# Second K and Q pieces on the SP and ACT queues, V first on GpSimd's queue, and a last row block in three column parts

## The chip, the core and the metric

The kernel runs on one core of a Trainium2 chip. The core has five engines with an instruction list each, taken in order: TensorE (PE; its weight loads are shown as PEld), VectorE (DVE), ScalarE (ACT), GpSimd (POOL) and SyncE (SP). They wait for one another by semaphores. Loads and stores are carried by 16 DMA engines that all queues share. GpSimd's queue is a software one (its instruction writes the descriptors and keeps it busy); the SP and ACT queues are hardware ones. The metric is the device time of one execution in microseconds, median of several.

## What is computed

A sliding-window attention over 8 batches, 8 heads, 576 tokens and head size 64, then a feed-forward layer with squared ReLU over its 4608 rows of 512:

```
scores = q @ k.T / 8,  masked to |i - j| <= 32
attn   = softmax(scores);  x = attn @ v          # heads side by side: 4608 x 512
h      = x @ w_in                                # 4608 x 2048
out    = (max(h, 0) ** 2) @ w_out                # 4608 x 512
```

Inputs and output are float32 in HBM; the matmuls run in bf16.

## The kernel before

The class `Gen` records operations, and the class `Prog` orders them. `Prog.rec` notes an operation's engine, its function, what it reads and writes, a sort key, a duration guessed in ns (`dur`), and for a transfer its packets (`move`: packets per DMA engine, ns of each, extra latency). `Prog.schedule` runs a list-scheduling model (`forward`, L98) forward and backward under several settings, keeps the best order, and `emit` writes one list per engine. So a changed duration or a changed key can move any operation of any engine. Operations with keys at or below -100 keep the order of their keys; the loads at the start have such keys, from the string `ORDER` (L34), in which `k01` is piece 1 of K of batch 0, `w10` the first quarter of `w_in` and `w20` that of `w_out`.

`fill` (L306) puts matmuls of zeros (L409) into the gaps that the plan has on TensorE up to about 30 us; `EXTRA` more of them stand before the first matmul of the first layer, which in the plan waits for `w10`.

Attention. K, Q and V come in pieces of tokens (`PIECE0`, L38, for K and Q of batch 0: 96, 64, 128, 128, 128, 32 tokens; `PIECE`, L39, for V). `tok_load` (L455) issues a K or Q piece on GpSimd's queue, float32 to bf16 on the way, 8 packets per token; `vx_load` (L526) does so for V. Piece 0 of K and Q of batch 0 is different: `first_load` (L448) issues it as float32 on the SP and ACT queues into two output buffers that are free then. `tok_turn` (L465) transposes a piece on TensorE into a PSUM bank and copies it to bf16 in SBUF, K by VectorE, Q by ScalarE; the float32 piece is transposed in float32 with a float32 identity, made by VectorE (L414) from an IOTA of GpSimd (L412). `scores`, `av`, `evac` and `xturn` then do a chunk of 64 tokens: scores, exponential, mask, weighted V, division, and the transpose of the result into `XT`. For the first eight chunks TensorE does these steps with one or two chunks at a time.

Feed-forward. `load_w1` (L544) and `load_w2` (L549) issue the weights in quarters on GpSimd's queue. `mm1_small` (L756; matmuls at L766) multiplies 128 rows by a quarter of `w_in` in 16 matmuls of 128 columns; `mm1_half` and `mm1` do wider ones later. ScalarE applies the ReLU and VectorE squares. `mm2` (L846) multiplies a block of 128 rows by `w_out` in four segments of 4 matmuls, ScalarE copies the 512 columns out of PSUM, and ACT's queue stores them. The last of the 36 row blocks goes to `last` (L825): two halves of 256 columns in two segments of 8 matmuls each; the first half is copied by ScalarE and stored by ACT's queue, the second copied by VectorE and stored by SP's:

```
        h, s = divmod(seg, 2)
        op, tag = ((self.OUTP[1][:, 0:256], ("outp", 1)), (self.BK["A"][:, 0:256], "sA"))[h]
```

GpSimd's list at the start is: IOTA, k01, q01, v00, v01, k02, q02, v02, w10, k03, q03, v03, k04, q04, v04, w11, w12, w13 and so on.

Of the kernel before, what the change touches and what calls it, by code (L numbers as in the profile page):

```python
# [19 lines left out]
VS = D_ + 2  # L20
KW = 32 + S_ + 32
LEAD = 12
WARM, COLD, DENSE, SPARSE, EXTRA = 36000, 8000, 1.15, 0.95, 16
NPE = 18
TB, TX = 1, 5
TOFF, TST = 6, 0.9
# [4 lines left out]
PADS, MARGINS, ROUNDS, NREP = (0, 1000, 2000), (0, 4000, 8000), 3, 4  # L31
LATE = {"POOL": 1500, "SP": 2000, "ACT": 2000}
DEPTH, POST, BACK = 4000, {"POOL": 1500, "SP": 1000, "ACT": 1000}, {"POOL": 2500, "SP": 4000, "ACT": 4000}
ORDER = ("k01 q01 v00 v01 k02 q02 v02 w10 k03 q03 v03 k04 q04 v04 w11 w12 w13 k05 q05 k10 q10 v10 k11 q11 v11 "  # L34
         "w20 w21 w22 w23 k12 q12 v12 k13 q13 v13 k14 q14 v14").split()
GT0, WT0 = (12.5, 16, 20, 25.5), (13, 18, 23, 26)
TURN0 = {1: 1, 2: 2, 4: 3, 6: 4}
# [10 lines left out]
class Prog:  # L48
# [49 lines left out]
    def forward(self, key=None, seq=None, rnd=None, pad=0):  # L98
# [3 lines left out]
        ready = [0.0] * n  # L102
        start, end = [0.0] * n, [0.0] * n
        free = {e: 900.0 for e in ENGS}
        free["POOL"] = 1350.0
        wait = {e: [] for e in ENGS}
        pool = {e: [] for e in ENGS}
        at = {e: 0 for e in ENGS}
# [250 lines left out]
class Gen:  # L359
# [5 lines left out]
    def alloc(self):  # L365
        nc = self.nc
        sb, ps = nc.alloc_sbuf_tensor, nc.alloc_psum_tensor
        self.SC = ps("sc", [128, 2048], F32)
        self.BK = {x: self.SC[:, 512 * i:512 * i + 512] for i, x in enumerate("ACBD")}
        self.TRP = self.BK["D"].bitcast(BF16)  # L370
        self.HT = [ps(f"ht{i}", [128, 512], F32) for i in range(2)]
        self.OUTP = [ps(f"outp{i}", [128, 512], F32) for i in range(2)]

        self.RAW = {t: [sb(f"{t}raw{i}", [128, 2560], BF16) for i in range(2)] for t in "qk"}
        self.QT = [sb(f"qt{i}", [128, 4, S_], BF16) for i in range(2)]
        self.KT = [sb(f"kt{i}", [128, 4, KW], BF16) for i in range(2)]
        self.VD = [sb(f"vd{i}", [128, 4, H_, VS], BF16) for i in range(2)]
        self.KA = [sb(f"ka{i}", [128, 4, 3, 128], BF16) for i in range(2)]
        self.VX = [sb(f"vx{i}", [128, 5, H_, VS], BF16) for i in range(2)]
        self.MASK = sb("mask", [128, 64], BF16)  # L380
        self.MASK2 = sb("mask2", [128, 2, 64], BF16)
        self.IOTA = sb("iota", [128, 256], mybir.dt.int32)
        self.IDW = sb("identw", [128, 256], BF16)
        self.ID = self.IDW[:, 64:192]
        self.MK = sb("mk", [128, 64], F32)
        self.E = sb("e", [128, 2048], BF16)
        self.PT = sb("pt", [128, 3 * 768], BF16)
        self.RS = [sb(f"rs{i}", [128, 16], F32) for i in range(4)]
        self.XR = sb("xr", [128, 4, 512], BF16)
        self.PF = sb("pf", [128, 16 * VE], F32)  # L390
        self.XT = sb("xt", [128, 4, NTOK], BF16)
        self.W1 = sb("w1", [128, 4, DFF], BF16)
        self.W2 = sb("w2", [128, 16, DM], BF16)
        self.GT = [sb(f"gt{i}", [128, 16, 512], BF16) for i in range(2)]
        self.RT = [sb(f"rt{i}", [128, 512], BF16) for i in range(4)]
        self.ZZ = sb("zz", [128, 128], BF16)
        self.OE = [sb(f"oe{i}", [128, 512], F32) for i in range(4)]
        self.STG = {"k": (self.OE[0], ("oe", 0)), "q": (self.OE[1], ("oe", 1))}
        self.IDF = self.OE[3][:, 0:128]


# [8 lines left out]

    def setup_masks(self, key):
        self.p.rec("POOL", lambda e: e.iota(self.IOTA[:], [[1, 256]], base=0, channel_multiplier=-1), writes=["iota"],  # L412
                   key=key, dur=400)
        self.p.rec("DVE", lambda e: e.tensor_scalar(self.IDF, self.IOTA[:, 0:128], 0.0, None, ALU.is_equal),  # L414
                   reads=["iota"], writes=[("oe", 3)], key=key - 0.1, dur=200)
        self.p.rec("DVE", lambda e: e.tensor_scalar(self.IDW[:], self.IOTA[:], 64.0, None, ALU.is_equal),
                   reads=["iota"], writes=["id"], key=key, dur=330)
        self.p.rec("DVE", lambda e: e.tensor_scalar(self.MK[:], self.IOTA[:, 0:64], -64.0, None, ALU.is_ge),
                   reads=["iota"], writes=["mk"], key=key + 0.1, dur=130)
        self.p.rec("DVE", lambda e: e.scalar_tensor_tensor(self.MASK[:], self.IOTA[:, 0:64], 0.0, self.MK[:], ALU.is_le,  # L420
                                                           ALU.mult),
                   reads=["mk", "iota"], writes=["mask"], key=key + 0.1, dur=130)
        self.p.rec("DVE", lambda e: e.tensor_scalar(self.MASK2[:, 0, :], self.IOTA[:, 0:64], -64.0, None, ALU.is_le),
                   reads=["iota"], writes=[("mask2", 0)], key=-20, dur=130)
        self.p.rec("DVE", lambda e: e.tensor_scalar(self.MASK2[:, 1, :], self.IOTA[:, 0:64], 0.0, None, ALU.is_ge),
                   reads=["iota"], writes=[("mask2", 1)], key=-20, dur=130)
# [18 lines left out]
    def slot(self, b, x):  # L445
        return 512 * (x if b else x - 1)

    def first_load(self, t, eng, key):  # L448
        t0, n = PIECE0[0]
        src = (self.q if t == "q" else self.k)[0, :, t0:t0 + n, :].rearrange("h p d -> p h d")  # L450
        stg, tag = self.STG[t]
        dst = bass.AP(stg, 0, [[512, n], [64, 8], [1, 64]])
        self.p.rec(eng, lambda e: e.dma_start(dst, src), writes=[tag], dma=(f"s{t}", 0), key=key, dur=420, move=(n // 2, 14, 1500))

    def tok_load(self, b, t, x, key):  # L455
        t0, n = self.pieces(b)[x]
# [2 lines left out]
        y = x - 1 if not b else x  # L459
        self.p.rec("POOL", lambda e: e.dma_start(dst, src), writes=[("fraw", b, t, x)], old=[("fraw", b - 2, t, y + (b == 2))],  # L460
                   reads=self.pace(b, x, "kqv".index(t)), dma=(f"f{b % 2}{t}{y}", b), key=key,
                   dur=500 + 3.2 * n, move=(n // 2, 13.3, (0, 1500, 800, 800, 800, 800)[x] if b == 0 else 200))
        self.p.ops[-1].slack = SLACK if b >= FB else 0

    def tok_turn(self, b, x, key):  # L465
        t0, n = self.pieces(b)[x]
        early = b == 0 and x < 3
        first = b == 0 and x == 0
        if b == 0 and x == 1:
            parts = [(t, "s" + u, self.BK[u].bitcast(BF16)) for t, u in ("kB", "qD")]  # L470
        elif early:
            parts = [(t, ("ht", u), self.HT[u][:] if first else self.HT[u][:].bitcast(BF16)) for u, t in enumerate("kq")]
        elif b:
# [8 lines left out]
        def f(e, todo):  # L482
            for t, tag, ps in todo:
                for j in range(4):
                    src = bass.AP(self.STG[t][0], 128 * j, [[512, n], [1, 128]]) if first else bass.AP(
                        self.RAW[t][b % 2], self.slot(b, x) + 128 * j, [[2560, n], [1, 128]])
                    mm = e.transpose(ps[:, 128 * j:128 * j + n], src, self.IDF[0:n, 0:n] if first else self.ID[0:n, 0:n])  # L487
            return mm

        for todo in ([parts[:1], parts[1:]] if early else [parts]):  # L490
            rd = [self.STG[t][1] for t, _, _ in todo] + [("oe", 3)] if first else [("fraw", b, t, x) for t, _, _ in todo]
            self.p.rec("PE", lambda e, a=todo: f(e, a), reads=rd + ["id"],
                       writes=sorted({tag for _, tag, _ in todo}), key=key, dur=450 if first else 240 * len(todo), att=True)
        if b == 0 and x == 3:
# [49 lines left out]
    def load_w1(self, d, key):  # L544
        src = self.w_in[:, 512 * d:512 * d + 512].rearrange("(f p) c -> p f c", p=128)
        self.p.rec("POOL", lambda e: e.dma_start(self.W1[:, :, 512 * d:512 * d + 512], src),  # L546
                   writes=[("w1", d)], dma=(f"w1{d}", 0), key=key, dur=770, move=(32, 82, 500))

    def load_w2(self, d, key):  # L549
        src = self.w_out[512 * d:512 * d + 512, :].rearrange("(k p) c -> p k c", p=128)  # L550
# [273 lines left out]

    def last(self, seg, key):  # L825
        gt = self.GT[(NT - 1) % 2]
        h, s = divmod(seg, 2)
        op, tag = ((self.OUTP[1][:, 0:256], ("outp", 1)), (self.BK["A"][:, 0:256], "sA"))[h]

        def f(e):  # L830
            for d in range(8 * s, 8 * s + 8):
                mm = e.matmul(op, gt[:, d, 384:512], self.W2[:, d, 256 * h:256 * h + 256], start=(d == 0), stop=(d == 15))  # L832
            return mm

        self.p.rec("PE", f, reads=[("gt", (NT - 1) % 2, d, 3) for d in range(8 * s, 8 * s + 8)] + [("w2", 2 * s), ("w2", 2 * s + 1)],
                   writes=[tag], key=key, dur=854)
        if s:
            oe = self.OE[3 * h][:, 0:256]
            if h:
                self.p.rec("DVE", lambda e: e.tensor_copy(oe, op), reads=[tag], writes=[("oe", 3)], key=key, dur=330)  # L840
            else:
                self.p.rec("ACT", lambda e: e.activation(oe, op, ACTF.Copy), reads=[tag], writes=[("oe", 0)], key=key, dur=400)
            self.p.rec("SP" if h else "ACT", lambda e: e.dma_start(self.out[NTOK - 128:NTOK, 256 * h:256 * h + 256], oe),
                       reads=[("oe", 3 * h)], writes=[("out", -h)], dma=(f"oz{h}", 0), key=key, dur=400, move=(8, 50))

    def mm2(self, T, u, seg, key):  # L846
        x = 4 * T + u
# [41 lines left out]
    def build(self):  # L889
# [18 lines left out]
        for b in range(B_):  # L908
# [2 lines left out]
                tile += 1  # L911
            if b < FB:
                if not b:
                    self.first_load("k", "SP", -300)
                    self.first_load("q", "ACT", -300)
                for bb in range(0 if b else FB):
                    for x in range(6):
                        for t in "kqv":
# [105 lines left out]
```

## Time and profile before

| | us |
|---|---|
| median of 6 runs (lowest, highest) | 303.65 (302.44, 304.67) |
| the profiled execution's own time | 304.46 |
| its span, first to last instruction | 302.6 |
| TensorE busy | 294.7 (97%) |
| VectorE, ScalarE, GpSimd busy | 177.9, 159.5, 106.7 |
| first piece of K, of Q landed (hardware queues) | 4.13, 4.44 |
| k01, q01, v00, v01 landed | 4.93, 5.35, 6.70, 7.81 |
| k02, q02, v02 landed | 8.98, 10.22, 11.10 |
| w10 issued, landed | 7.07, 16.34 |
| k03, q03, w11, w12, w13 landed | 17.19, 18.07, 23.77, 26.30, 28.85 |
| last matmul ends, last store issued | 300.02, 300.61 |

Times count from the span's start. A load has landed when the last of its 16 completions, one per DMA engine, has come. In the profile's lines, "x16" counts instructions, "out<-in" names what is written and read by the program's names without buffer numbers, and the bracket at the end of a line of the timeline gives the idle time of the engine before it and what ended it. The granted TensorE clock was 0.999 over the span. A busy TensorE includes the matmuls of zeros (120 in this execution, all before 15 us).

### The profile page before, as it was taken

To read this page: it belongs to the slowest core of one execution; us is meant where nothing else is said; L and a number is where in the kernel's file an instruction comes from. 1 tells how busy PE (TensorE), PEld (TensorE's weight loads), DVE (VectorE), ACT (ScalarE), POOL (GpSimd) and SP (SyncE) were. 2 spreads that over 40 slices of the span, in tenths; PEclk is the share of its full clock that TensorE was granted. 3 is DMA by queue.
4 is the path that set the end of the run, shared out by engine and by line. 5 is a ranking of instruction groups with operands and counts; after the bars stand their busy time and mean duration, and the time that the engine had idled before them with its cause. 6 is when DMAs were issued, how large, how long until landed. Compare 5 with 4: busy or idle time off the path is not lost.

```text
span 302.6 us, 7056 instructions
## 1 busy us (share of the span) xinstructions
PE 294.7 (97%) x2786; PEld 172.0 (57%) x2786; DVE 177.9 (59%) x429; ACT 159.5 (53%) x266; POOL 106.7 (35%) x133
## 2 busy tenths in 40 slices
PE   8869999999999999999999999999999999999996
PEld 8759965775858764544544444444454444444444
DVE  6666657754998966658566496758447663222200
ACT  3356644574747645754565674647464554444311
POOL 8999914240604631552055544315510000000000
PEclk9999999999999999999999999999999999999999
DMA  9999999999999999999899999999992310100022
GB/s 111 152 187 176 200 179 174 175 135 163 186 156 134 140 169 160 143 129 146 152 130 131 151 168 160 124 175 95 163 161 72 87 26 35 37 35 36 35 96 79
DMA packets 166673, 39.07 MB, mean 129 GB/s; under 512 B 157808, under 2 KB 162160, under 8 KB 166640
## 3 DMA queue, kind: packets, MB, share of 16 engines
q0 software_dynamic: 115200, 18.16, 89.3%
q1 hardware_dynamic: 45472, 10.96, 24.5%
q10 hardware_dynamic: 5968, 9.51, 10.3%
q8 instruction: 22, 0.36, 0.5%
q14 instruction: 11, 0.09, 0.1%
HBM read 36.70 MB, written 9.44 MB: 152 GB/s over the span
## 4 chain that ended last, share of the span: by engine, by line
PE 91%; POOL 4%; DMA 4%; issue 0%; DVE 0%; DVEq 0%; POOLq 0%
PE outp L855 40%; PE ht L807 28%; PE ht L789 7%; PE ht L766 7%; DMA w<-in_moe_w_in_dram 4%; PE sc L643 3%; PE sc L583 3%; POOL vx L529 1%; POOL kraw L460 1%; POOL qraw L460 1%; PE sc L487 1%; PE sc L832 1%; PE outp L832 1%; PE sc L691 0%; POOL w L546 0%
## 5 line engine op out<-in xcount | busy, mean ns | idle before, releaser
L855 PE MATMUL outp<-w,gt 128*128 128x512 bf16 x560 | 136.0, 379 | 0.0
L807 PE MATMUL ht<-xt,w 128*128 128x512 bf16 x384 | 94.5, 379 | 0.0
L822 DVE TENSOR_TENSOR gt<-rt 128x512 bf16<-128x512 bf16 x144 | 59.1, 418 | 58.0 <-ACT rt L813 50.9
L813 ACT ACTIVATE rt<-ht 128x512 bf16<-128x512 f32 x96 | 57.3, 599 | 56.7 <-PE ht L807 54.6
L855 PEld LDWEIGHTS outp<-w,gt 128*128 128x128 bf16 x560 | 52.7, 98 | 58.3 <-DVE gt L822 0.2
L807 PEld LDWEIGHTS ht<-xt,w 128*128 128x128 bf16 x384 | 36.5, 98 | 42.4
L460 POOL DMA_DIRECT2D qraw<-in_q_dram x40 | 34.7, 868 | 53.6 <-DVE xr L667 12.7
L460 POOL DMA_DIRECT2D kraw<-in_k_dram x40 | 34.9, 873 | 43.0 <-PE ht L807 19.1
L603 ACT ACTIVATE e<-sc 128x512 bf16<-128x512 f32 (+1 forms) x48 | 37.4, 810 | 11.5 <-PE sc L583 11.5
L529 POOL DMA_DIRECT2D vx<-in_v_dram x40 | 34.7, 868 | 19.0 <-PE ht L807 11.6
L862 ACT ACTIVATE oe<-outp 128x512 f32<-128x512 f32 x35 | 20.9, 598 | 26.7 <-PE outp L855 26.6
L667 DVE TENSOR_TENSOR xr<-pf,rs 128x512 bf16<-128x512 f32 (+1 forms) x42 | 27.7, 681 | 0.4
L766 PE MATMUL ht<-xt,w 128*128 128x128 bf16 x384 | 24.1, 219 | 2.4 <-DMA w<-in_moe_w_in_dram 2.0
L624 DVE TENSOR_TENSOR pt<-e,mask 128x512 bf16<-128x512 bf16 x42 | 17.6, 421 | 13.9 <-ACT e L603 13.8
L789 PE MATMUL ht<-xt,w 128*128 128x256 bf16 x192 | 23.4, 273 | 0.0
L766 PEld LDWEIGHTS ht<-xt,w 128*128 128x128 bf16 x384 | 21.7, 98 | 3.0 <-issue 1.7
L774 ACT ACTIVATE rt<-ht 128x512 bf16<-128x512 f32 x24 | 14.2, 599 | 13.3 <-PE ht L766 13.1
L660 DVE COPY pf<-sc 128x520 f32<-128x520 f32 x21 | 14.7, 698 | 11.1 <-PE sc L643 10.9
L789 PEld LDWEIGHTS ht<-xt,w 128*128 128x128 bf16 x192 | 18.0, 98 | 3.3
L657 ACT ACTIVATE pf<-sc 128x520 f32<-128x520 f32 x21 | 12.6, 600 | 12.3 <-PE sc L643 11.0
L795 ACT ACTIVATE rt<-ht 128x512 bf16<-128x512 f32 x24 | 14.4, 599 | 7.5 <-PE ht L789 6.8
L662 DVE TENSOR_TENSOR pf<-pf 64x520 f32<-64x520 f32 x21 | 14.6, 697 | 5.5 <-ACT pf L657 4.7
(80 smaller groups left out, 193.6 us busy)
## 6 DMA issues: line engine op xcount, KB each, us to landing
out_dram<-oe ACTq DMA_DIRECT2D x35, 256.0 KB, 3.7
kraw<-in_k_dram POOLq DMA_DIRECT2D x31, 128.0 KB, 5.3
qraw<-in_q_dram POOLq DMA_DIRECT2D x31, 128.0 KB, 5.5
vx<-in_v_dram POOLq DMA_DIRECT2D x24, 128.0 KB, 5.3
w<-in_moe_w_in_dram POOLq DMA_DIRECT2D x4, 512.0 KB, 11.6
w<-in_moe_w_out_dram POOLq DMA_DIRECT2D x4, 512.0 KB, 18.0
vx<-in_v_dram POOLq DMA_DIRECT2D x16, 96.0 KB, 5.3
xt<-xr SPq DMA_TRANSPOSE x36, 4.4
```

The source lines that it names most:

```text
L460: self.p.rec("POOL", lambda e: e.dma_start(dst, src), writes=[("fraw", b, t, x)], old=[("fraw", b - 2, t, y + (b == 2))], reads=self.pace( ...
L529: self.p.rec("POOL", lambda e: e.dma_start(self.VX[b % 2][r:r + n, s, :, 0:64], self.v[b, :, t0:t0 + n, :].rearrange("h p d -> p h d")), w ...
L603: self.p.rec("ACT", lambda e, d=dst, a=src: e.activation(d, a, ACTF.Exp, scale=0.125), reads=["s" + x for x in name], writes=[("e", h)], k ...
L624: self.p.rec("DVE", lambda e, a=pt, c=ee, d=mb: e.tensor_tensor(a, c, d, ALU.mult), reads=[("e", k // 2), "mask"], writes=[("ptt", k)], ol ...
L667: self.p.rec("DVE", lambda e, w=w, np=np: e.tensor_tensor(bass.AP(self.XR, 512 * (2 * y + w), [[2048, np], [64, 2], [128, 4], [1, 64]]), b ...
L766: mm = e.matmul(ht[:, 128 * (d % 4):128 * (d % 4) + 128], self.W1[:, ft, 128 * d:128 * d + 128], self.XT[:, ft, t0:t0 + 128], start=(ft == ...
L789: mm = e.matmul(ht[:, 256 * (d % 2):256 * (d % 2) + 256], self.W1[:, ft, 128 * d:128 * d + 128], self.XT[:, ft, 64 * s0:64 * s0 + 256], st ...
L807: mm = e.matmul(ht[:], self.W1[:, ft, 128 * d:128 * d + 128], self.XT[:, ft, 512 * T:512 * T + 512], start=(ft == 0), stop=(ft == 3))
L813: self.p.rec("ACT", lambda e: e.activation(rt[:], ht[:], ACTF.Relu), reads=[("ht", k % 2)], writes=[("rt", k % 4)], key=key, dur=560)
L822: self.p.rec("DVE", lambda e: e.tensor_tensor(g, r, r, ALU.mult), reads=[("rt", k % 4)], writes=tags, key=key, dur=430)
L855: mm = e.matmul(op, gt[:, d, 128 * u:128 * u + 128], self.W2[:, d, :], start=(d == 0), stop=(d == 15))
L862: self.p.rec("ACT", lambda e: e.activation(oe[:], op, ACTF.Copy), reads=[tag], writes=[("oe", x % 4)], key=key, dur=560)
```

## The change

K and Q of piece 1 of batch 0 (tokens 96 to 159) leave GpSimd's list. `first_load` now takes the piece as an argument and is called for pieces 0 and 1: both K pieces on SP's queue, both Q pieces on ACT's. Piece 1 lands as float32 in the buffer `PF`, which attention uses later, and `tok_turn` transposes it in float32 like piece 0. GpSimd's list begins with v00; the IOTA's key puts it between v00 and v01. The planner's constants change with this: GpSimd is free at 850 ns in place of 1350, w10's packets cost 130 ns in place of 82, and 6 extra matmuls of zeros stand before the first layer in place of 16. The last row block is done as 256 columns in two segments of 8 matmuls, then 128 columns in 16 matmuls and 128 in 16: the first two parts are copied by ScalarE and stored by ACT's queue, the last is copied by VectorE and stored by SP's.

```
-WARM, COLD, DENSE, SPARSE, EXTRA = 36000, 8000, 1.15, 0.95, 16
+WARM, COLD, DENSE, SPARSE, EXTRA = 36000, 8000, 1.15, 0.95, 6
...
-ORDER = ("k01 q01 v00 v01 k02 q02 v02 w10 k03 q03 v03 k04 q04 v04 w11 w12 w13 k05 q05 k10 q10 v10 k11 q11 v11 "
+ORDER = ("v00 v01 k02 q02 v02 w10 k03 q03 v03 k04 q04 v04 w11 w12 w13 k05 q05 k10 q10 v10 k11 q11 v11 "
...
-        free["POOL"] = 1350.0
+        free["POOL"] = 850.0
...
-        self.STG = {"k": (self.OE[0], ("oe", 0)), "q": (self.OE[1], ("oe", 1))}
+        self.STG = {("k", 0): (self.OE[0], 0, 512, ("oe", 0)), ("q", 0): (self.OE[1], 0, 512, ("oe", 1)),
+                    ("k", 1): (self.PF, 0, 16 * VE, ("pf", 0)), ("q", 1): (self.PF, 512, 16 * VE, ("pf", 1))}
...
         self.p.rec("POOL", lambda e: e.iota(self.IOTA[:], [[1, 256]], base=0, channel_multiplier=-1), writes=["iota"],
-                   key=key, dur=400)
+                   key=-198.5, dur=400)
...
-    def first_load(self, t, eng, key):
-        t0, n = PIECE0[0]
+    def first_load(self, t, x, eng, key):
+        t0, n = PIECE0[x]
...
-        stg, tag = self.STG[t]
-        dst = bass.AP(stg, 0, [[512, n], [64, 8], [1, 64]])
-        self.p.rec(eng, lambda e: e.dma_start(dst, src), writes=[tag], dma=(f"s{t}", 0), key=key, dur=420, move=(n // 2, 14, 1500))
+        stg, o, w, tag = self.STG[t, x]
+        dst = bass.AP(stg, o, [[w, n], [64, 8], [1, 64]])
+        self.p.rec(eng, lambda e: e.dma_start(dst, src), writes=[tag], dma=(f"s{t}{x}", 0), key=key, dur=420, move=(n // 2, 14, 1500))
...
-        first = b == 0 and x == 0
+        first = b == 0 and x < 2
         if b == 0 and x == 1:
-            parts = [(t, "s" + u, self.BK[u].bitcast(BF16)) for t, u in ("kB", "qD")]
+            parts = [(t, "s" + u, self.BK[u]) for t, u in ("kB", "qD")]
...
-                   writes=[("w1", d)], dma=(f"w1{d}", 0), key=key, dur=770, move=(32, 82, 500))
+                   writes=[("w1", d)], dma=(f"w1{d}", 0), key=key, dur=770, move=(32, 82 if d else 130, 500))
...
     def last(self, seg, key):
...
-        h, s = divmod(seg, 2)
-        op, tag = ((self.OUTP[1][:, 0:256], ("outp", 1)), (self.BK["A"][:, 0:256], "sA"))[h]
+        if seg < 2:
+            lo, w, op, tag, eng, ds = 0, 256, self.OUTP[1][:, 0:256], ("outp", 1), "ACT", range(8 * seg, 8 * seg + 8)
+        else:
+            bank, eng = (("A", "ACT"), ("C", "DVE"))[seg - 2]
+            lo, w, op, tag, ds = 128 * seg, 128, self.BK[bank][:, 0:128], "s" + bank, range(16)
...
+        if seg:
+            i = (0, 0, 1, 3)[seg]
+            oe = self.OE[i][:, 0:w]
+            if eng == "DVE":
+                self.p.rec("DVE", lambda e: e.tensor_copy(oe, op), reads=[tag], writes=[("oe", i)], key=key, dur=200)
             else:
-                self.p.rec("ACT", lambda e: e.activation(oe, op, ACTF.Copy), reads=[tag], writes=[("oe", 0)], key=key, dur=400)
-            self.p.rec("SP" if h else "ACT", lambda e: e.dma_start(self.out[NTOK - 128:NTOK, 256 * h:256 * h + 256], oe),
-                       reads=[("oe", 3 * h)], writes=[("out", -h)], dma=(f"oz{h}", 0), key=key, dur=400, move=(8, 50))
+                self.p.rec("ACT", lambda e: e.activation(oe, op, ACTF.Copy), reads=[tag], writes=[("oe", i)], key=key, dur=200 + w)
+            self.p.rec("ACT" if seg < 3 else "SP", lambda e: e.dma_start(self.out[NTOK - 128:NTOK, lo:lo + w], oe),
+                       reads=[("oe", i)], writes=[("out", -seg)], dma=(f"oz{seg}", 0), key=key, dur=400, move=(8, 50))
...
-                    self.first_load("k", "SP", -300)
-                    self.first_load("q", "ACT", -300)
+                    for x in range(2):
+                        self.first_load("k", x, "SP", -300 + x)
+                        self.first_load("q", x, "ACT", -300 + x)
```

## The prediction

> **What bounds the kernel now.** I read the page's slices first, then a table of stages, then TensorE's waits in the one stage where it is not full, and last the landing of each load. The stage table (busy us and instruction counts of PE, PE weight load, VectorE, ScalarE and GpSimd, then TensorE clock, DMA share, GB/s):
>
> ```profile
> 13.00:24.00 11.00, 7.33 (x150) 6.29 (x148) 6.64 (x15) 4.73 (x8) 11.00 (x16) 1.00 1.73 183
> 24.00:40.00 16.00, 16.00 (x294) 15.24 (x291) 9.92 (x28) 10.49 (x19) 13.45 (x17) 1.00 1.64 189
> ...
> 240.00:298.00 58.00, 58.00 (x292) 27.24 (x290) 16.50 (x38) 24.12 (x42) 0.00 (x0) 1.00 0.12 41
> 298.00:303.00 5.00, 2.02 (x19) 1.56 (x16) 0.42 (x1) 0.38 (x1) 0.00 (x0) 0.92 0.30 105
> ```
>
> From 24 to 300 us TensorE has no gap at full clock: no other engine's saving there can show. What is left is the head, where TensorE waits or multiplies zeros, and the tail after its last matmul. The fill matmuls of line 409 end at 14.9 us; the waits of TensorE between 14 and 25 us (total us, times, longest):
>
> ```profile
> PE ht L766 <- DMA w<-in_moe_w_in_dram: 2.0, 2, 1.6
> PE outp L747 <- DVE kt L503: 0.5, 1, 0.5
> PE sc L718 <- DVE pt L612: 0.4, 1, 0.4
> ```
>
> The 2.0 us are the waits for the first and second quarter of the first weight (w10, w11): 1.60 us up to 16.48 and 0.45 up to 23.81. So the head is set by when these land. The timeline shows where w10 stands in GpSimd's list:
>
> ```profile
> 0.83 0.33 POOL L412 IOTA iota<- 128x256 int32 x1 [0.39 <-POOLq L1009]
> ...
> 1.35 0.81 POOL L460 DMA_DIRECT2D kraw<-in_k_dram  x1 [0.19 <-issue]
> ...
> 2.16 0.68 POOL L460 DMA_DIRECT2D qraw<-in_q_dram  x1
> 2.82 1.67 POOL L529 DMA_DIRECT2D vx<-in_v_dram  x2
> ...
> 7.07 0.81 POOL L546 DMA_DIRECT2D w<-in_moe_w_in_dram  x1
> ...
> 16.48 1.05 PE L766 MATMUL ht<-xt,w 128*128 128x128 bf16 x16 [1.60 <-DMA w<-in_moe_w_in_dram]
> ```
>
> w10's sixteen completions run from 12.28 to 16.34 us: fourteen by 14.27, two late. From there each 1024-packet piece lands 0.84 us and each weight quarter 2.53 us after the one before, without a break to 45 us: one saturated stream. Whatever moves its front moves w10, the K and Q pieces behind it, w11 and so the moment at which TensorE becomes full.
>
> **The change part by part.** *GpSimd's list.* Two issues leave it (0.81 + 0.68 us). The first issue can start at 0.83, where the IOTA stands, but the IOTA then follows V's first piece. New times: v00 from 0.83, 0.78 us (its share of the x2 row) plus 0.13 (0.81 less 0.68, what the first issue took over the second) to 1.74; the IOTA's 0.33 and the 0.19 gap behind it to 2.26; v01, k02, q02, v02 at the 0.87 spacing of the trace to 5.74. There w10 is issued, 1.33 us before 7.07. The IOTA comes 0.9 us later; what waits for it is VectorE's identity (1.29 now, some 2.2 then), needed by the transposes at 4.48: cover 2.3 us, cost nothing.
>
> *The DMA engines.* The 2 x 512 packets of these pieces are not gone: they go to the SP and ACT queues, behind the 768 of each first piece. The packet records, counted in fifths of a microsecond, show 219 to 226 packets with both hardware queues full (2.8 to 3.2 us) and 205 to 239 with GpSimd's alone (6.6 to 9.2 us), so about 1,115 per us by either way. Between, GpSimd underfeeds them; DMA share is the column before the last:
>
> ```profile
> 5.00:6.00 1.00, 1.00 (x14) 0.90 (x13) 0.56 (x1) 0.12 (x1) 1.00 (x2) 1.00 1.40 89
> ...
> 8.00:9.00 1.00, 0.68 (x18) 0.47 (x15) 0.94 (x3) 0.60 (x1) 1.00 (x2) 1.00 2.19 139
> ```
>
> Ahead of w10 stand 1,536 hardware and 5,888 software packets, 7,424 before as after (2,560 and 4,864). By 9.2 us some 5,040 software ones are recorded, so the rest ends about 9.2 + 850/1,115 = 9.95 us. With the engines full from 2.6 us (469 packets are done by then) the same total ends at 2.6 + 6,955/1,115 = 8.85: 1.1 us earlier. That is less than GpSimd's 1.33, so the engines decide: **w10 and the stream behind it come 1.1 us earlier**. Ends for the range: 0.4 us if hardware and software packets mix no better than in 3.4 to 3.8 us (about 174 a fifth against 223, for the 1,024 moved packets: 1,024/870 - 1,024/1,115 = 0.26 us) and some dips stay (0.4); above, 1.33 us by GpSimd's issues. I take 1.1 because the dips fall at 4 to 6.4 us, just where the added hardware packets run.
>
> A rule weighed against this: the Trainium skill, Trainium Kernel Development and Optimization, Key Constraints, says that transfers from the SP, ACT and GpSimd queues share the same 16 DMA engines, and that issuing from several saves only the sequencer's issue time. Read strictly it speaks against a gain while the engines are full; by issue time alone the head would gain 1.33, by full engines nothing. The trace lies between, with 1.1 us of unfed time.
>
> *The late two engines.* w10 took the last engine 5.24 us (11.10 to 16.34) against 2.53 for w11; among its packets are single ones of 0.3 to 1.07 us beside the usual 98 ns. Nothing in the change touches that; it is put at nothing, with 0 to 1 us either way as the spread between executions.
>
> *The second pieces on chip.* They stay f32, so 8 transposes and two evacuations change form. Rows (f32 of 96 tokens, bf16 of 64, and their evacuations):
>
> ```profile
> 5.33 0.51 PE L487 MATMUL ht<-oe 96*128 96x96 f32 x4
> ...
> 6.44 0.29 PE L487 MATMUL sc<-identw,qraw 64*128 64x64 bf16 x4
> ```
>
> Each set of four costs 0.29 to 0.51 us, so 0 to 0.22 more, twice; VectorE's evacuation lies between 0.29 (256 bf16) and 0.56 us (384 f32 columns). The landing may be later: if hardware and software share evenly from 2.9 us, the hardware's remaining 1,900 packets end about 6.3 and q01 lands near 6.7 (5.35 now; its transpose runs at 6.44), and q00 some 0.5 us after its 4.44. All of it, at most 1.2 us, lies in the chain to the first transposed attention rows, which ScalarE finishes at 13.40, 2.9 us before w10 now and 1.8 after. Cost nothing; without that cover up to 1.2 us. Behind the second issue on ACT's queue (0.41 us) stands the table load, done at 2.47 and not needed before 5.88; SP has no further work there.
>
> *The plan.* All lists are planned anew with w10 costed 1.5 us longer (48 ns x 32), and 10 fewer trailing fills (0.5 us). Now fills end 1.6 us before w10, so they cost nothing and their loss nothing. What the new order is worth is not in the trace: bounded by the other waits between 16.5 and 23.8 us, 0.34 + 0.52 + 0.35 + 0.41 = 1.6 us gained at best, and by the worst rival below. I take 0: the stretch holds the same work.
>
> *The tail.* Rows:
>
> ```profile
> 298.11 1.91 PE L832 MATMUL sc<-w,gt 128*128 128x256 bf16 x16
> ...
> 300.15 0.42 DVE L840 COPY oe<-sc 128x256 f32<-128x256 f32 x1 [13.76 <-PE sc L832]
> 300.61 0.38 SPq L843 DMA_DIRECT2D out_dram<-oe  x1
> ```
>
> Sixteen 128-column matmuls take 0.89 us (L766, chain of waits), so two parts take 1.78 for 1.76: +0.02. The last copy falls from 256 to 128 columns: 698 ns at 520 columns and 425 at 256 give 1.03 ns each, so 0.13 less. Half the bytes in the last store, which lands 1.7 us after issue: 0 to 0.1 less, I take 0.05. The third part (ScalarE's copy, then ACT's queue, behind the first half's copy 0.38 and issue 0.34) is issued some 0.8 us before the last: hidden. Tail: 0.15 us less; bounds 0 and 0.25.
>
> **Sum.** 1.1 + 0.15 = 1.25 us. The profiled execution took 304.46 us (span 302.6 and 1.9 around it), 0.81 above the median of 303.65; the steps carry over to the median: 302.4, less 0.4%.
>
> **The rivals.** *The stalls behind w10 shrink too.* For it: 1.6 us of waits between w10 and w11, and a plan whose w10 is nearer to the real one. Against: they hang on the same stream. Time: 302.4 less up to 1.6, 300.8 to 301.6.
>
> *The engines were the bound anyway, or the late two decide.* Then the queues change and w10 does not: gain 0 to 0.6, 303.0 to 303.7. For it: 7,424 packets before and after, and two engines 1.2 to 2 us behind the rest; against: the unfed dips.
>
> *Slower: the order puts work that needs w11 in front of work that does not.* TensorE takes its list in order. Between w10 and w11 it now does three groups of first-layer matmuls (0.9 us each) and two pairs of attention chunks (some 0.4 + 0.25 + 0.25 us each): 4.5 us. A w11 group planned ahead of them would push up to that behind w11: 302.4 + 4.5 = 306.9 at worst. It decides against the change from 1.25 us pushed back, and shows as slower from 2.8. Against: in the plan, as on the chip, w11 stands behind all K and Q pieces of chunks 3 to 7.
>
> **How the numbers follow.** 0.5%, 1.5 us here, is about what a measurement of this kernel can tell from no change. Forecast (gain 0.7 to 2.0, that is 301.65 to 302.95, its own range): 0.53, of which 0.24 above 1.5 us, since the terms' upper ends add up to 1.6 and the late engines add up to 1. Stalls shrink too: 0.18, faster. No head gain: 0.14, same. Slower order: 0.15, of which 0.14 by over 0.5%. Faster 0.42, same 0.44, slower 0.14. For 8 in 10 the range goes from 300.8 (all upper ends and the 1.6 us, rounded) to 304.4, which leaves out most of the slower case and little of the fast one.
>
> **What would show it.** GpSimd's w10 issue near 5.7 us; packet rate without the dips at 4 to 6.4 us; w10's last completion near 15.2 and w11's near 22.7; TensorE full from about 22.7; the last copy 0.29 us and the last store landing 1.7 us after issue. It is wrong if w10 is issued earlier but lands at 16, if TensorE shows new waits between w10 and w11, or if gaps open after 24 us.

## The result and the profile after

The changed kernel takes 301.11 us (median of 17 executions, 301.02 to 303.75) against 303.37 us of the kernel before (36 executions, 301.95 to 304.96): 0.9933 of the time before, 95% interval 0.9918 to 0.9948, so 0.67% or 2.0 us less; the two medians differ by 2.26 us. The forecast was 302.4 us.

Twelve of the 17 executions lie between 301.0 and 301.4 us at a whole TensorE clock, and five lie 0.7 to 2.7 us above with a mean clock of 0.994 or 0.989, and the profiled one is the slowest of these, 303.75 us with a span of 301.9. What lowers the clock is one of the questions of the experiments below.

The stages of the changed kernel, columns as before (the TensorE clock is the third from the end):

```profile
7.00:13.00 6.00, 5.70 (x63) 4.75 (x64) 3.34 (x10) 2.16 (x4) 6.00 (x8) 0.55 1.89 173
13.00:24.00 11.00, 10.01 (x203) 9.09 (x201) 6.65 (x19) 5.62 (x10) 11.00 (x15) 0.93 1.66 190
24.00:40.00 16.00, 16.00 (x292) 15.12 (x289) 10.10 (x29) 10.87 (x19) 13.18 (x16) 1.00 1.64 188
```

TensorE is full from 24 us on, as before. The clock of 0.55 in the row of 7 to 13 us is new; the matmuls of the head run at half rate there. The waits of TensorE between 10 and 30 us:

```profile
PE outp L749 <- DVE kt L505: 0.5, 1, 0.5
PE ht L768 <- ACT xt L755: 0.3, 1, 0.3
```

The 2.0 us on the first weight are gone, although half clock stretched the list in front of it. Instead TensorE now waits for the second K piece. The timeline of the head, and the landing of w10 after its issue:

```profile
1.30 0.89 POOL L531 DMA_DIRECT2D vx<-in_v_dram  x1 [0.86 <-POOLq L1016]
...
2.27 0.37 POOL L413 IOTA iota<- 128x256 int32 x1
2.55 1.02 POOL L531 DMA_DIRECT2D vx<-in_v_dram  x1
...
6.17 0.79 POOL L548 DMA_DIRECT2D w<-in_moe_w_in_dram  x1
...
7.30 0.46 PE L489 MATMUL sc<-oe,pf 64*128 64x64 f32 x4 [1.33 <-DMA pf<-in_k_dram]
...
DMA to landing us min/median/max: 6.9/6.9/6.9
```

w10 is issued 0.90 us earlier than before (7.07) and lands at 13.02, 3.3 us earlier than the 16.34 of the profile before. The tail:

```profile
297.71 1.95 PE L837 MATMUL sc<-w,gt 128*128 128x128 bf16 x32
...
299.70 0.29 DVE L846 COPY oe<-sc 128x128 f32<-128x128 f32 x1 [13.71 <-PE sc L837]
300.01 0.36 SPq L849 DMA_DIRECT2D out_dram<-oe  x1
```

From the end of the last matmul to the end of the span it is 301.94 - 299.66 = 2.28 us, 2.63 before.

### The profile page after: what moved, and what is told of

Its sections match the earlier page's. It is cut to its first block, busy times and chain, and to the rows that moved or that the text cites. A ratio compares the mean times of both kernels' runs of the same rounds, so it can differ in the third digit from the quotient of the medians.

```text
span 301.9 us, 7075 instructions
## 1 busy us (share of the span) xinstructions
PE 296.2 (98%) x2793; PEld 173.9 (58%) x2793; DVE 175.8 (58%) x429; ACT 160.1 (53%) x267; POOL 105.8 (35%) x131
## 4 chain that ended last, share of the span: by engine, by line
PE 96%; DMA 2%; ACT 1%; DVE 0%; issue 0%; SPq 0%
PE outp L861 40%; PE ht L809 28%; PE ht L768 7%; PE ht L791 7%; PE sc L585 4%; PE sc L645 3%; DMA pf<-in_k_dram 2%; PE outp L410 2%; PE sc L489 1%; PE sc L837 1%; PE outp L837 1%; PE sc L693 0%; PE sc L720 0%; PE outp L749 0%; PE sc L721 0%; PE ht L489 0%
## 5 line engine op out<-in xcount | busy, mean ns | idle before, releaser
L461 POOL DMA_DIRECT2D qraw<-in_q_dram x39 | 33.4, 857 | 51.0 <-PE ht L809 24.2
L461 POOL DMA_DIRECT2D kraw<-in_k_dram x39 | 33.5, 859 | 45.1 <-PE ht L809 18.6
L605 ACT ACTIVATE e<-sc 128x512 bf16<-128x512 f32 (+1 forms) x48 | 37.5, 810 | 13.2 <-PE sc L585 13.2
L776 ACT ACTIVATE rt<-ht 128x512 bf16<-128x512 f32 x24 | 14.3, 598 | 10.5 <-PE ht L768 10.2
L659 ACT ACTIVATE pf<-sc 128x520 f32<-128x520 f32 x21 | 12.6, 601 | 11.9 <-PE sc L645 11.9
L797 ACT ACTIVATE rt<-ht 128x512 bf16<-128x512 f32 x24 | 14.4, 600 | 7.3 <-PE ht L791 6.7
## 6 DMA issues: line engine op xcount, KB each, us to landing
w<-in_moe_w_out_dram POOLq DMA_DIRECT2D x4, 512.0 KB, 16.3
```

Of the source, the lines that this page charges most:

```text
L605: self.p.rec("ACT", lambda e, d=dst, a=src: e.activation(d, a, ACTF.Exp, scale=0.125), reads=["s" + x for x in name], writes=[("e", h)], k ...
```

## The experiments

Three theories run through them. A is the prediction's: the first layer starts when w10 lands. B: in the changed kernel w10 is early, and TensorE's own list, with its matmuls of zeros, sets the start of the first layer. C: the tail or the plan carries the gain. D was formed from the profile above: the wait for the second K piece brings the halved clock.

### The changed kernel again

No edit.

> The changed kernel once more, for the profile of an execution near its median of 301.1 us: the profiled one took 303.75 at a TensorE clock of 0.989. Theory A (the prediction's): the first layer starts when w10 has landed, with a wait of TensorE on w10 before it, and w10 lands near 15.2 us. Theory B (w10 no longer ends last): w10 lands near 13 us as in the slow profile, TensorE goes from matmuls of zeros straight into the first layer, and nothing waits for a weight. Either: span near 299.3 at clock 1.0, with the first layer some 2 us earlier than the 17.2 us of the slow profile.

It took 304.1 us, again with the low clock. Its stages from 4.5 to 24 us:

```profile
4.50:7.00 2.50, 1.34 (x15) 0.99 (x12) 1.60 (x11) 0.49 (x1) 2.50 (x4) 1.00 2.13 161
7.00:13.00 6.00, 5.49 (x61) 4.49 (x62) 2.87 (x9) 1.87 (x4) 6.00 (x8) 0.56 1.93 176
13.00:24.00 11.00, 10.06 (x200) 9.03 (x199) 7.85 (x20) 5.71 (x9) 11.00 (x15) 0.93 1.63 191
```

So there is no profile of an execution at 301.1 us, but the rest supports B: w10 landed at 12.55, and the first layer came at 17.42 straight out of the matmuls of zeros. The record of the granted clock has it at half from 7.74 us for 6.83 us, two stretches of 3.41 us, right after a stretch of 3.41 us in which TensorE had stood still for 1.6 us. From the first layer to the end it is 302.28 - 17.42 = 284.9 us here and 301.94 - 17.22 = 284.7 in the profile above. An execution at 301.1 us has a span of some 299.3 us, so its first layer starts near 14.5 us, if it takes as long from there; that is an estimate (in the two padded kernels below, profiled at whole clock, the first layer starts at 14.54 and 14.20, and it is 285.3 and 285.0 from there).

### The tail alone, and all but the tail

The kernel before with the new `last`, and the changed kernel with the old one.

> The kernel before with the new last row block alone. Theory A and B: 0.15 us less than before (0 to 0.25), not to be told from no change; the last copy takes 0.29 us in place of 0.42 and the last store lands 1.7 us after its issue. If the tail carried the gain (theory C): 1 us or more less.

> The changed kernel with the old last row block. Theory A and B: 0.15 us above the changed kernel, about 301.25 us, still some 2.1 us faster than before. Theory C: back near 303 us.

The tail alone: 303.3 us, 0.9993 (0.997 to 1.0016), no difference that can be told. Without the tail: 301.41 us, 0.9933 (0.991 to 0.9956), fastest 301.32 against 301.02. C falls for the tail; the two runs allow it 0.2 to 0.3 us. From the last matmul to the end the profiles of all runs give 2.28 to 2.36 us with the new tail and 2.53 to 2.63 with the old.

The profile of the tail alone is also a second look at the head of the kernel before: v02's last completion is at 13.22 in place of 11.10, w10's at 15.74, and TensorE stands still for 2.23 us before 14.41. The first layer comes at 17.06, well after w10, and it is 284.8 us from there to the end. Which of the late engines strikes what differs between executions.

### Twenty more matmuls of zeros before the first layer

```
-WARM, COLD, DENSE, SPARSE, EXTRA = 36000, 8000, 1.15, 0.95, 6
+WARM, COLD, DENSE, SPARSE, EXTRA = 36000, 8000, 1.15, 0.95, 26
```

> The changed kernel with 20 more matmuls of zeros (54 ns each, 1.1 us) just before the first layer, EXTRA 26 for 6, the order of everything else unchanged. Theory A: they end before w10 lands, so no change, 301.1 us. Theory B: TensorE goes straight from them into the first layer, so the first layer comes 1.1 us later; the time rises by up to 1.1 us, to 302.2, less what TensorE waits for w11 and the pieces behind it now.

303.22 us, 0.9987 (0.9964 to 1.001); the executions at whole clock start at 302.46, 1.4 us above those of the changed kernel in the result and 1.1 above the fastest without the tail on the same chip; the median is 1.0 above the 302.2 that was the most expected. The first layer in the changed kernel's repeat, and here:

```profile
17.19 0.39 PE L410 MATMUL outp<-zz 128*128 128x128 bf16 x4
17.42 1.06 PE L768 MATMUL ht<-xt,w 128*128 128x128 bf16 x16
```

```profile
17.14 1.50 PE L410 MATMUL outp<-zz 128*128 128x128 bf16 x24
18.48 1.06 PE L768 MATMUL ht<-xt,w 128*128 128x128 bf16 x16
```

The 20 matmuls push the first layer back by 1.06 us, about what they take (1.50 us for 24 against 0.39 for 4), and w10 had landed 6 us before (12.36). A falls for the changed kernel; B stands.

### w10 held back on GpSimd

```
+        def f(e):
+            if not d:
+                for u in range(4):
+                    e.iota(self.JUNK[:, 256 * u:256 * u + 256], [[1, 256]], base=0, channel_multiplier=-1)
+            return e.dma_start(self.W1[:, :, 512 * d:512 * d + 512], src)
```

> The changed kernel, all lists in the same order, with four IOTAs into an unused buffer just before GpSimd issues w10, which delays w10 and all behind it by some 1.3 us of GpSimd's time and, as the engines have packets waiting, by 0.5 to 1.3 us at the landing (13.0 to 13.5-14.3 us). Theory A (the first layer waits for w10): the time rises by the same 0.5 to 1.3 us, to 301.6 to 302.4. Theory B (TensorE's own list with its matmuls of zeros sets the first layer at about 14.6 us, w10 is early): rise below 0.4 us.

The issue of w10 and its landing:

```profile
6.18 1.26 POOL L552 IOTA junk<- 128x256 int32 x4
7.34 0.81 POOL L553 DMA_DIRECT2D w<-in_moe_w_in_dram  x1
...
DMA to landing us min/median/max: 5.8/5.8/5.8
```

w10 is issued 0.27 us later than in the kernel before and still lands at 13.11, 3.2 us earlier, within 0.1 us of the 13.02 of the profile after (13.5 to 14.3 was expected). So the time at which GpSimd issues w10 is not what made w10 early; the pieces ahead of it were issued as early as in the changed kernel here, so of their issue times this says nothing. The time is less clear: 303.14 us, 0.9961 (0.9932 to 0.9989), with six of ten executions at a lowered clock; the four at whole clock take 301.57 to 301.95 and 303.89, where the changed kernel's at whole clock take 301.0 to 301.4 in the result and 301.2 to 301.7 beside the last experiments, on other chips. That is near the border between A and B, and without the changed kernel on the same chip it decides nothing. No wait for w10 appears in the profile, which speaks for B.

### V first alone

The kernel before with the new order and the new place of the IOTA, the second K and Q pieces still on GpSimd's queue:

```
-ORDER = ("k01 q01 v00 v01 k02 ...
+ORDER = ("v00 v01 k01 q01 k02 ...
...
-                   key=key, dur=400)
+                   key=-198.5, dur=400)
...
-        free["POOL"] = 1350.0
+        free["POOL"] = 850.0
```

> The kernel before with V first and the IOTA behind v00, the second K and Q pieces still on GpSimd's queue behind v01. Theory A: w10 is issued 0.4 us earlier than before at most and stands behind the same 7,424 packets, so w10 lands as before (15.5 to 16.5 us) and the time is 303 us, within 0.5 us of before. If V first carried the gain: near 301 us.

304.03 us, 0.9996 (0.997 to 1.0022): nothing. The timeline of GpSimd says why:

```profile
1.29 0.89 POOL L529 DMA_DIRECT2D vx<-in_v_dram  x1 [0.85 <-POOLq L1009]
2.26 0.37 POOL L412 IOTA iota<- 128x256 int32 x1
2.55 1.02 POOL L529 DMA_DIRECT2D vx<-in_v_dram  x1
...
7.61 0.77 POOL L546 DMA_DIRECT2D w<-in_moe_w_in_dram  x1
```

The first transfer starts at 1.29 whether an IOTA stands before it or not (1.35 with it), so the IOTA was free in its old place and is not in its new one: w10 is issued 0.54 us later than before, and lands at 15.60. What makes w10 early is thus the move of the two pieces to the other queues, not the order on GpSimd's.

### The second K piece later in the plan

```
-  ... dma=(f"s{t}{x}", 0), key=key, dur=420, move=(n // 2, 14, 1500))
+  ... dma=(f"s{t}{x}", 0), key=key, dur=420, move=(n // 2, 14, 3100 if (t, x) == ("k", 1) else 1500))
```

> The changed kernel with the extra latency of the second K piece set to 3100 ns in the planner (1500 before), near its landing at 7.3 us: the plan puts the first scores and the second Q piece ahead of the second K piece's transposes. Theory B with D (the wait of 1.0 to 1.6 us for that piece at 7.3 us is the new head-of-line wait, and the halved TensorE clock of about 4 to 7 us behind it makes the slow executions): the wait shrinks below 0.7 us, the clock stays whole, executions above 301.5 us get rarer, and the median is 301.1 or up to 0.5 us less. Theory A: no change in the fast executions, since w10 decides.

The wait for the piece falls to 0.4 us, and the clock is whole in the profile. But the median is 302.62 us, 0.9939 (0.9914 to 0.9965), well above the 301.1 expected, and four of the twelve executions have a mean clock of 0.994. Their heads were not profiled, so these four neither support D nor refute it. In the profile the first layer is as early as 14.44, and then TensorE waits again:

```profile
14.44 1.06 PE L768 MATMUL ht<-xt,w 128*128 128x128 bf16 x16
15.33 1.06 PE L410 MATMUL outp<-zz 128*128 128x128 bf16 x16
17.49 0.28 PE L410 MATMUL outp<-zz 128*128 128x128 bf16 x2 [1.10 <-issue]
17.61 0.39 PE L489 MATMUL outp<-identw,kraw 128*128 128x128 bf16 x4
```

K's piece 4, for which TensorE transposes next, landed at 17.26: one DMA engine again (the fifteenth completion came at 15.84). An earlier first layer is worth only as much as the pieces behind it follow.

### Fewer matmuls of zeros

```
-WARM, COLD, DENSE, SPARSE, EXTRA = 36000, 8000, 1.15, 0.95, 6
+WARM, COLD, DENSE, SPARSE, EXTRA = 36000, 8000, 1.15, 0.60, 0
```

> The changed kernel with fewer matmuls of zeros (density 0.60 for 0.95 after 8 us, none of the 6 extra ones: 24 fewer, 1.3 us at full clock), the order of everything else unchanged. Theory A: no change. Theory B: up to 1.3 us less where TensorE then waits for nothing else, so 299.8 to 301.1 us; more executions with a lowered clock are possible, as TensorE is idle more often.

The fastest execution takes 300.66 us, 0.4 less than the changed kernel's on another chip; the median is 301.86, 0.9926 (0.99 to 0.9952), and nine of twelve executions have the lowered clock. That fits B, and taking the matmuls away alone is no gain that can be told. The next section has the cleaner comparison, on one chip and at whole clock.

### Matmuls of zeros where TensorE waits for the second K piece, alone and with fewer behind

The third kernel joins this edit and the one above:

```
+            if b == 0 and x == 1 and todo[0][0] == "k":
+                self.p.pad = self.p.ops[-1]
...
-... (EXTRA if op is self.first and op.start < self.idle_end.start else 0)
+... (EXTRA if op is self.first and op.start < self.idle_end.start else 20 if op is self.pad else 0)
```

> The changed kernel again, on the same chip as the three below. All theories: 0.993 of the kernel before, most executions within 0.3 us of one another and some 0.7, 1.5 or 2.7 us above, with a mean clock of 0.994 or 0.989.

> The changed kernel with 20 matmuls of zeros just before the transposes of the second K piece, where TensorE waits 1.0 to 1.6 us at 7.3 us; they take 1.1 us and end near 7.1, before the piece lands. Theory D (that idle stretch brings the halved clock): the clock stays whole, the executions at 0.994 and 0.989 vanish, the fast ones stay as they are, so the median is that of the changed kernel's fast executions, 301.1 us, and the highest below 301.8. Against D: slow executions as often as in the changed kernel, or the matmuls run late at half clock and cost up to 1 us.

> The same 20 matmuls of zeros before the second K piece, and the thinner ones behind it (density 0.60, none of the 6 extra). Theories B and D together: 0.4 us below the fast executions of the changed kernel, as the fastest of fewer_fills showed (300.66 for 301.02), so 300.7 us, without slow ones. If the thinner matmuls let the clock fall: some executions 0.7 us or more above.

On this chip the changed kernel took 301.70 us, 0.995 (0.9925 to 0.9974), four of twelve executions with a lowered clock, the highest 304.60. With the 20 matmuls: 301.83 us, 0.9938 (0.9917 to 0.9958), all eight at whole clock (the profile shows it by its matmuls of zeros, 56 ns apart before and behind the piece), the highest 302.46 (below 301.8 was expected). The median did not fall, but the executions with a lowered clock are gone. With both edits: 300.96 us, 0.9911 (0.9886 to 0.9936), all six at whole clock, 300.45 to 301.18; the fastest version here, 0.7 us below the changed kernel beside it, though the two intervals still touch. The two padded kernels have the same instructions in the same order but for the 24 matmuls of zeros taken out: every execution with fewer lies below every one with more (300.45 to 301.18 against 301.21 to 302.46), the medians by 0.87 us, at whole clock throughout. So these matmuls cost time, as B says. The head of the fastest version:

```profile
5.96 1.39 PE L410 MATMUL outp<-zz 128*128 128x128 bf16 x22
7.38 0.46 PE L489 MATMUL sc<-oe,pf 64*128 64x64 f32 x4
```

```profile
4.50:7.00 2.50, 2.50 (x32) 2.49 (x31) 1.60 (x11) 0.49 (x1) 2.50 (x4) 1.00 2.19 158
7.00:13.00 6.00, 5.57 (x106) 4.41 (x104) 4.72 (x13) 3.10 (x5) 6.00 (x8) 1.00 1.91 174
```

The second row against that of the repeat: the same stretch with the clock at 1.00 for 0.56, and 106 matmuls done for 61. The piece landed no earlier (7.34). So D stands for this wait: it is the idle stretch, not the late piece as such, that brought the lowered clock. It is not the only place where the clock can fall: without any second piece on these queues, three of the twelve executions of the tail alone and two of the ten of V first alone have a mean clock of 0.994; they were not profiled. The first layer starts at 14.20.

### The old constants of the planner

The changed kernel with EXTRA 16 and 82 ns for w10's packets.

> The changed kernel with the planner's old constants for w10 (82 ns a packet) and EXTRA 16: the loads as in the changed kernel, TensorE's order planned for an earlier w10. Theory B: w10 still lands near 12.6 us; the first layer moves with TensorE's list (0.5 us more zeros before it, planned 0.4 us earlier), so 301.0 to 301.8 us. If the planner's constants carried the gain: near 303 us.

302.47 us, 0.9957 (0.9936 to 0.9978), with five of twelve executions at a lowered clock and the fastest at 301.0. TensorE's order is another one, and w10 landed at 14.11 by a single late engine (the fifteenth at 12.26). The time is above the 301.0 to 301.8 expected. By the medians it keeps 1.3 us of a gain of 2.1; whether the new constants are worth the 0.8 us between it and the changed kernel beside it can't be told (0.995, the intervals overlap).

## Why the prediction was right, and where not

The direction and the place were right; the gain was 2.0 us by the ratio and 2.3 between the medians, for 1.25. 301.11 us lies in the wide range (300.8 to 304.4) but below the forecast's own (301.65 to 302.95), where the rival "stalls shrink too" stood. That it came no lower is luck in part: w10 came 2 us earlier than predicted (13.02 for 15.2), and the first layer could not use all of it. Of the other signs, w11 landed at 20.50 for 22.7, and the dips of the packet rate became shallower without going away (from 4 to 6.4 us, 163 to 244 packets a fifth of a microsecond for 88 to 197).

*The front of the stream: right in sum.* v02, the last piece before w10, had its last completion at 11.10 and has it at 9.90 now (9.8 to 10.5 in the other profiles with the new queues): 1.2 us for the 1.1. One reading in the sum is wrong: 5,040 software packets are about those recorded by 9.0 us (5,020); by 9.2 us it is 5,243, and the same sum then gives 0.9 us. Two other errors pulled against each other. Mixed hardware and software packets ran at 163 to 192 a fifth of a microsecond from 4 to 5.6 us, the lower end that the prediction kept for its range; the software ones behind them ran at 235 to 246 from 6 to 8.6 us, above the 198 to 239 before (packets by their start, those of 4 bytes left out).

*GpSimd's list: wrong by 0.4 us.* w10's issue was to come at 5.74 and came at 6.17, as the first issue could not start at 0.83. V first alone is worth nothing, and w10 held back past its old issue time still landed early, so w10's own issue did not count. For the pieces ahead of it, the runs do not tell saved issue time from packets that ran in unfed time: v02 was issued 0.90 us earlier (5.30 for 6.20) and its fourteenth completion came 0.95 us earlier (9.71 for 10.66), and in V first alone it was issued 0.45 us later and its last completion came 0.41 us later. So the rule that the prediction weighed (the Trainium skill, Trainium Kernel Development and Optimization, Key Constraints: issuing from several queues saves only issue time) is neither shown nor contradicted here: in the unfed time, 5 to 6 us before, GpSimd was issuing without a break (busy 1.00 of 1.00 us).

*The late two engines, put at nothing: the step that failed.* The prediction let w10 keep its 5.24 us on the last engine and shifted it by 1.1. It takes 3.1 us now (9.90 to 13.02), and 2.4 to 3.0 in nine of the ten other profiles with the new queues (4.3 in the tenth, with the old constants); in the old head it took 5.24 and 4.1 us, and 2.5 after a v02 that was late itself. Among w10's 512 packets, 18, 9 and 15 took over 250 ns in the three profiles with the old head, 0 to 2 in nine with the new queues, 4 with the old constants, 7 with w10 held back. So w10 landed at 12.3 to 13.1 us (14.1 with the old constants) in place of 15.6 to 16.3, not 1.1 us earlier but 2.5 to 4, and w11 landed at 20.3 to 21.6 in place of 23.2 to 23.8. No packet of another load took as long in the first 30 us. Why single packets of the first weight are slow in the old head stays open: w10 held back has seven of them, though its packets begin at 8.9 us as in the other profiles with the new queues (8.5 to 9.0; 9.2 to 9.9 in the old head), so the time of reading alone does not explain them. One candidate was not tested: each profile has a 16 KB packet of the queue that the page lists as q8, instruction, which takes one DMA engine 0.94 to 0.98 us. In the head it starts at 12.6 to 13.6 us in the three old heads and at 12.74 with the old constants, before w10 has landed, and at 13.2 to 15.5 in the ten others, after it has. The trace does not say which engine carries it; at its length it could be a part of the lag, not all of it.

*What took the gain back.* Of those 3 us the first layer could use only a part, since TensorE's list was not ready: B, with the matmuls of zeros in it. The path on which the prediction rests, from w10's landing to the first layer, held in the profile before (16.34 and 16.48) and not in ten of the eleven with the new queues (w10 at 12.3 to 13.1, the first layer at 14.20 or later). The two profiles, before and after, add up like this. Before, from the first layer to the end, 302.65 - 16.48 = 286.2 us; after, 284.7. Of these 1.45 us, 1.1 are waits between the first layer and 24 us (2.07 before: 0.34, 0.52, 0.35, 0.41, 0.45; 0.99 after: 0.52, 0.35, 0.12), and 0.35 the tail. The shorter waits are the rival "stalls shrink too", beside the forecast's own term and not in place of it. The rest of the 2.26 us, some 0.8, is the earlier first layer: estimated at 14.5 now, and at 301.5 - 286.2 = 15.3 by the median before less 1.9 us. The split is no more than an estimate, since the two parts trade against each other: the later the first layer, the shorter the waits behind it (17.06 and 284.8 us to the end in the tail alone, 15.74 and 286.5 in V first alone), and the profile after has a first layer that the half clock made late.

*The second pieces, at nothing: half right.* Both landings and cover were in the prediction, with 6.7 us for the later one. SP's second piece landed at 7.26 (7.46 and 8.12 in two more executions), ACT's at 5.83; in other executions ACT's was the late one (7.09, 7.14). The cover was the time until w10, and that went with w10's early landing; whether the 1.33 us of waiting cost anything at whole clock is not shown, since the changed kernel was profiled only at the lowered clock (with the piece later in the plan, the wait was 0.4 us and the first layer came at 14.44, no earlier than estimated). What the prediction also missed is that idle time there has a second price: a halved clock for 3.4 or 6.8 us, 0.7 to 2.7 us of the end in about a third of the executions.

*The tail: mis-sized.* 0.15 was taken, the two profiles give 0.35 from the last matmul's end: 0.13 for the copy as predicted (0.42 to 0.29), 0.11 for the landing (1.73 to 1.62 us) in place of 0.05, and 0.1 between the modelled end of the last matmul and the copy (0.14 to 0.04). This last part is scatter and not the change: it is 0.14 with the new tail in the tail alone and 0.04 with the old one in V first alone. So the tail is worth 0.24.

*The slower rival* had nothing for it: no work on w11 stands in front, and no gap opens after 24 us.

## What to carry to other kernels

A load that everybody waits for is done when the last DMA engine is done: look at its sixteen completions, not at its issue, before working out what moving it is worth, and treat an engine that lags in one execution as a term with a size of its own. When a wait is taken out, ask what stands in the list in front of it; here matmuls of zeros that had stood in a wait before the change cost most of their time after it. And a short wait in a head that has just warmed up may cost more than its length: putting the same matmuls of zeros into that wait, and thinning them where they no longer cover one, gave the fastest version here.

## What the runs showed of the hardware

The TensorE clock can halve after a wait that is quite short. The granted clock changes in steps of 3.41 us. In the profile after, in the stretch from 4.22 to 7.63 us, TensorE stood still for 1.33 us at once (1.46 in all), and the clock was half for the next 6.83 us; with 0.96 us of standing still (no tail) it was half for 3.41 us; filled with matmuls it stayed whole. The Trainium skill, TensorE: Matmul & The Clock Gate, Part 1 (the HAM clock gate), gives a free-running window of 3413 ns, which the steps confirm, and an idle window of that length as what brings the half clock; here about 1 us within one window was enough.

The same length of standing still later was not enough: 1.60 us before w10 (14.9 to 16.5) in the profile before, and 2.23 us in that of the tail alone (12.2 to 14.4), left the clock whole. What separates the two in all 13 profiles that have clock records is whether the wait falls in the first stretch of whole clock, that is right after the moment, 4.0 to 6.6 us into the span, at which the matmuls of zeros go from 107 ns apart to 56. In seven profiles TensorE stood still for 0.96 to 1.67 us in that first stretch, and in all seven the clock was half in the next one: for 3.41 us after 0.96 and 1.07 us, for 6.83 us after 1.46 to 1.67. In the other six it stood still there for at most 0.63 us, and the clock stayed whole, with up to 1.49 us of standing still in a later stretch. The place within the stretch does not explain it: with the second K piece later in the plan, 1.10 us at the end of a later stretch (16.39 to 17.49 of 14.20 to 17.61 us) left the clock whole. No run moved one wait from the first stretch to a later one and changed nothing else.

With two hardware transfers issued one behind the other on each of two queues, the second ones do not share evenly: after the first pieces, one queue's second piece got most of the engines and the other's 0 to 4 packets a fifth of a microsecond for 0.6 us, then 19 to 93 beside the software ones (3.6 to 5.4 us in the profile after). Either queue can be the loser.

GpSimd's first transfer starts at 1.29 to 1.35 us even with nothing in front of it, so the IOTA of 0.33 us before it was free, and behind it the next issue came at 2.55 us.
